# Where the load of w_out stands in GpSimd's queue of loads

## The chip, the cores and the metric

The kernel runs on one core of a Trainium2 chip. The metric is the time of one execution on the device, in microseconds (us). The median of three runs of the kernel before is 156.59 us, the lowest is 156.43 and the highest 156.64.

## The reference

An attention layer with a sliding window and four sink positions feeds a gated MLP block whose gate mixes along the sequence. There are 4 batches of 768 positions, 8 heads of 64 values, so 512 model columns, and twice 512 columns inside the MLP. Cut to what matters:

```python
scores = scale * (q @ k.T)                      # per batch and head, 768 x 768
keep = (pos_k < 4) | ((0 <= pos_q - pos_k) & (pos_q - pos_k < 128))
a = softmax(where(keep, scores, -1e9))
x = concat_heads(a @ v)                         # 768 x 512 per batch

h = gelu(x @ w_in)                              # 768 x 1024
u, v = h[:, :512], h[:, 512:]
v_n = (v - mean(v)) / sqrt(var(v) + 1e-6) * g_ln
v_s = w_sg @ v_n + b_sg[:, None]                # mixes the 768 positions
out = x + (u * v_s) @ w_out
```

## The kernel before

Everything is cut into 128 positions (a tile, six of them in a batch) and 128 columns. The four batches, numbered 0 to 3, go through the same steps, and the steps of neighbouring batches are interleaved by hand. The order is the string `STEPS`: the program walks through it, and each word calls the function of that name with the numbers behind the dots. The last letter, where there is one, is the engine: A for ScalarE (ACT), D for VectorE (DVE), P for GpSimd (POOL). A scheduler changes nothing of it. Each engine gets its own instructions in the order of the string, runs them strictly in that order, and waits on semaphores where an instruction needs something that another engine or a DMA has still to deliver.

These are the steps that the text speaks of. `b` is the batch, `p` a pair of heads (0 to 3).

- `LQ.b.t` and `LK.b.t` (issued in `load`, L223, for batches 1 and 2) load tile t of q or k of a batch, all heads: 1024 runs of 64 values, turned from float32 to bfloat16 on the way, 128 KB in SBUF. `LVH.b.i` (L269) loads v of four heads, 384 KB in SBUF. `LWO` (L283) loads all of w_out, 512 KB in SBUF, 512 runs of 512 values. All of these are issued by POOL and go through one software queue that the 16 DMA engines serve.
- `TQ.b.g` and `TK.b.g` (L377) turn two tiles of q or k on TensorE (PE); `EQ` and `EK` copy the result to SBUF. `TK.2.1` needs the key tiles `LK.2.2` and `LK.2.3`, `TQ.2.1` needs the query tiles `LQ.2.2` and `LQ.2.3`, `TK.2.2` needs `LK.2.4` and `LK.2.5`.
- `QK.b.p.g` (L478) makes scores on PE, `EX.b.p.g` (L483) takes their exponential on ACT, `MK.b.p.g` masks the result: one multiplication on DVE (L490), or two selections on POOL (L493 and L496).
- `AV.b.p.k` (L519, L523, L526) multiplies the masked weights by v for one half of the positions. For batch 1, `AV.1.p.1` covers tiles 3, 4 and 5 with five matmuls each; from tile 4 on it reads what `MK.1.p.2` has masked. `NR` (L535, L536) divides by the sums.
- `SP`, `GT` and `GM` (L622, L627, L632) make the gate; `GM.0.1.2.P` is one of its products on POOL.
- `OU.b.t` (L639) is the last matmul of a tile and the only reader of w_out. `OU.0.0` is the first of them. `RA` adds x to it on DVE, `ST` stores the sum.

The tile framework gives POOL's loads eight completion semaphores in turn, and a load waits at its issue until the load that used its semaphore before has landed. That is the eighth POOL load before it. As long as the loads before it land in time, nobody sees this wait.

In the part of the string around the change, each of the engines concerned has this order before the change:

- POOL: `LK.2.1 LVH.1.0 LVH.1.1 LQ.2.2 LWO LK.2.2 LK.2.3 LQ.2.3 LQ.2.4 LQ.2.5 GM.0.0.2 LK.2.4 LK.2.5 MK.1.1.2 MK.1.0.2 MK.1.2.2 MK.1.3.2 GM.0.1.2 LK.3.0 GM.0.1.3 GM.0.1.1 LVH.2.0 ...`
- PE, from its 52nd microsecond on: `... AV.1.2.0 AV.1.3.0 QK.2.0.0 QK.2.1.0 OU.0.0 TK.2.1 AV.1.0.1 AV.1.1.1 AV.1.2.1 AV.1.3.1 QK.2.2.0 QK.2.3.0 OU.0.1 OU.0.2 TK.2.2 TQ.2.1 TQ.2.2 MV.1.0 ...`

Of the kernel before, what the change touches and what calls it, by code (L numbers as in the profile page):

```python
# [30 lines left out]
WE.0.A WT.1 GV.0.2 LK.1.5 TK.1.1 MU.0.2 LB.P EK.1.1.A BN.0.2 Z.0.0.A LK.2.0 WT.2 GU.0.2 MU.0.0 WE.1.D RS.0.2 WE.2.D  # L31
Z.0.1.A LQ.2.0 NM.0.2 Z.0.2.A Z.0.3.D Z.0.4.D WT.3 LQ.2.1 WT.4 GU.0.0 WE.3.D WT.5 LQ.1.4 Z.0.5.D TQ.1.1 QK.1.0.0
EQ.1.1.D QK.1.1.0 LQ.1.5 SP.0.0.0 WE.4.D LK.2.1 EX.1.0.0 VSM.1 SP.0.0.1 WE.5.D EX.1.1.0 LVH.1.0 GT.0.0.0 TK.1.2 KS.1
GT.0.0.1 QK.1.2.0 QK.1.3.0 EX.1.2.0 SP.0.0.2 LVH.1.1 GM.0.0.0.D EX.1.3.0 MK.1.2.0.D TQ.2.0 EK.1.2.A LQ.2.2 QK.1.0.1
EQ.2.0.D QK.1.1.1 TQ.1.2 EX.1.0.1 GT.0.0.2 LWO SP.0.0.3 EQ.1.2.D EX.1.1.1 LK.2.2 MK.1.0.1.D TK.2.0 MK.1.0.0.D QK.1.2.1
LK.2.3 EK.2.0.A QK.1.3.1 MK.1.3.0.D SK.1.0 GM.0.0.1.D LQ.2.3 SP.0.1.0 EX.1.2.1 GT.0.0.3 MK.1.1.0.D LQ.2.4 EX.1.3.1
SP.0.1.1 MK.1.1.1.D LQ.2.5 MK.1.2.1.D SX.1.0 QK.1.0.2 QK.1.1.2 GT.0.1.0 EX.1.0.2 GM.0.0.2.P SP.0.1.2 GT.0.1.1 EX.1.1.2
LK.2.4 GM.0.1.0.D AV.1.0.0 MK.1.3.1.D AV.1.1.0 LK.2.5 GM.0.0.3.D QK.1.2.2 GT.0.1.2 QK.1.3.2 EX.1.2.2 SP.0.1.3 NR.1.0.0
MK.1.1.2.P EX.1.3.2 NR.1.1.0 AV.1.2.0 AV.1.3.0 MK.1.0.2.P GT.0.1.3 QK.2.0.0 QK.2.1.0 NR.1.2.0 EX.2.0.0 OU.0.0
MK.1.2.2.P NR.1.3.0 TK.2.1 RA.0.0 AV.1.0.1 XD.1.0 EK.2.1.A MK.1.3.2.P AV.1.1.1 NR.1.0.1 AV.1.2.1 EX.2.1.0 GM.0.1.2.P  # L40
NR.1.1.1 AV.1.3.1 NR.1.2.1 QK.2.2.0 LK.3.0 QK.2.3.0 EX.2.2.0 OU.0.1 NR.1.3.1 GM.0.1.3.P EX.2.3.0 OU.0.2 XD.1.1 RA.0.1
GM.0.1.1.P TK.2.2 MK.2.3.0.D TQ.2.1 LVH.2.0 TQ.2.2 EQ.2.1.D MV.1.0 EQ.2.2.D LQ.3.0 EK.2.2.D LQ.3.1 VSM.2 MU.1.0 GV.1.0
# [668 lines left out]
```

## Time and profile before

| | |
|---|---|
| median of 3 runs | 156.59 us |
| the profiled execution | 157.69 us |
| its span, first instruction to last | 156.0 us |
| PE busy | 146.7 us, 94% of the span |
| DVE, ACT, POOL busy | 123.4, 99.0, 99.3 us |
| granted TensorE clock | 9 tenths or more in each of 40 slices |
| software queue's share of 16 DMA engines | 94.9% |
| share of w_out's load in the chain that ended last | 7% |

The profile is of one execution. Times in it count from the start of its span, and 1.69 us of the execution lie outside that span. PE's busy time is modelled for the ends of its matmuls, so a PE that is busy is not a PE at its peak. The page lists, for groups of instructions, the idle time of the engine just before them and what ended it; the chain of waits goes back from the last instruction to whatever released each one.

### The profile page before, as it was taken

To read this page: it belongs to the slowest core of one execution; us is meant where nothing else is said; L and a number is where in the kernel's file an instruction comes from. 1 tells how busy PE (TensorE), PEld (TensorE's weight loads), DVE (VectorE), ACT (ScalarE), POOL (GpSimd) and SP (SyncE) were. 2 spreads that over 40 slices of the span, in tenths; PEclk is the share of its full clock that TensorE was granted. 3 is DMA by queue.
4 is the path that set the end of the run, shared out by engine and by line. 5 is a ranking of instruction groups with operands and counts; after the bars stand their busy time and mean duration, and the time that the engine had idled before them with its cause. 6 is when DMAs were issued, how large, how long until landed. Compare 5 with 4: busy or idle time off the path is not lost.

```text
span 156.0 us, 3856 instructions
## 1 busy us (share of the span) xinstructions
PE 146.7 (94%) x1549; PEld 94.2 (60%) x1549; DVE 123.4 (79%) x295; ACT 99.0 (64%) x110; POOL 99.3 (64%) x127
## 2 busy tenths in 40 slices
PE   6988989999999979989999999999999999999990
PEld 2445577779675756747566764486567644776530
DVE  4557789829989969969789887899789956867981
ACT  3699798799899846276897855269954025591000
POOL 4099779388999899997549869640798610300400
PEclk9999999999999999999999999999999999999999
DMA  4999999999999999999999199995710580510064
GB/s 156 282 365 151 153 197 189 166 192 193 146 143 142 193 152 139 167 156 156 168 230 246 22 285 174 178 197 60 236 71 3 102 235 0 202 63 11 0 227 179
DMA packets 86170, 24.67 MB, mean 158 GB/s; under 512 B 78660, under 2 KB 83016, under 8 KB 86152
## 3 DMA queue, kind: packets, MB, share of 16 engines
q0 software_dynamic: 64608, 11.01, 94.9%
q1 hardware_dynamic: 21544, 13.41, 33.1%
q8 instruction: 12, 0.20, 0.5%
q14 instruction: 6, 0.05, 0.1%
HBM read 24.81 MB, written 6.29 MB: 199 GB/s over the span
## 4 chain that ended last, share of the span: by engine, by line
PE 73%; DMA 17%; DVE 2%; POOL 2%; issue 1%; ACT 1%; SPq 1%; ACTq 0%
PE mm L622 17%; PE mm L639 14%; PE sc L561 13%; PE sc L602 12%; DMA w_out_sb<-in_moe_w_out_dram 7%; DMA v_sb<-in_v_dram 6%; PE sc L478 4%; DMA uT<-in_k_dram 4%; PE mm L519 3%; PE mm L377 3%; PE mm L523 2%; PE mm L526 2%; PE mm L614 1%; POOL v_sb L269 1%; PE mm L545 1%
## 5 line engine op out<-in xcount | busy, mean ns | idle before, releaser
L483 ACT ACTIVATE P<-sc 128x1024 bf16<-128x1024 f32 (+1 forms) x48 | 43.4, 953 | 10.3 <-PE sc L478 10.1
L622 PE MATMUL mm<-wsgT,z 128*128 128x384 bf16 x192 | 34.1, 327 | 0.0
L622 PEld LDWEIGHTS <-z 128*128 128x128 bf16 x192 | 17.7, 98 | 11.9 <-issue 0.7
L639 PE MATMUL mm<-w_out_sb,wsg_gated 128*128 128x512 bf16 x96 | 22.7, 379 | 1.1 <-DMA w_out_sb<-in_moe_w_out_dram 1.1
L561 PE MATMUL sc<-w_in_sb,xT 128*128 128x512 bf16 x96 | 22.2, 379 | 0.7 <-ACT vt L565 0.7
L627 DVE SCALAR_TENSOR_TENSOR gtmp<-mm,g_sb,b_bc 128x384 bf16<-128x384 f32 x32 | 19.1, 611 | 4.2 <-PE mm L622 3.6
L602 PE MATMUL sc<-xT,w_in_sb 128*128 128x256 bf16 x192 | 22.1, 273 | 0.0
L493 POOL TENSOR_SCALAR_AFFINE_SELECT P<-P 128x512 bf16<-128x512 bf16 x21 | 14.0, 667 | 12.3 <-ACT P L483 12.0
L632 POOL TENSOR_TENSOR wsg_gated<-gtmp,uT 128x384 bf16<-128x384 bf16 x15 | 14.5, 982 | 10.9 <-DVE gtmp L627 10.9
L574 DVE BATCH_NORM_STATS2 st<-vt 128x6 f32<-128x512 f32 x24 | 15.4, 685 | 7.5 <-ACT vt L565 7.4
L602 PEld LDWEIGHTS <-w_in_sb 128*128 128x128 bf16 x192 | 18.7, 98 | 3.0
L536 DVE TENSOR_TENSOR x_sb<-mm,rcp 128x384 bf16<-128x384 f32 (+1 forms) x36 | 18.5, 513 | 1.2
L643 DVE TENSOR_TENSOR ot<-mm,x_sb 128x512 f32<-128x512 f32 x24 | 16.1, 684 | 2.7 <-PE mm L639 2.5
L565 ACT ACTIVATE vt<-sc 128x1024 f32<-128x1024 f32 x12 | 12.3, 1027 | 9.0 <-PE sc L561 8.9
L583 POOL TENSOR_TENSOR rs<-rs,neg_half 128x4 f32<-128x4 f32 (+1 forms) x8 | 6.9, 867 | 17.4 <-DVE rs L578 16.0
L223 POOL DMA_DIRECT2D k<-in_k_dram x18 | 16.4, 928 | 0.7 <-DMA v_sb<-in_v_dram 0.7
L223 POOL DMA_DIRECT2D q<-in_q_dram x18 | 16.7, 952 | 0.0
L519 PE MATMUL mm<-v_sb,P 128*128 128x65 bf16 x192 | 15.9, 194 | 0.7 <-DMA v_sb<-in_v_dram 0.6
L519 PEld LDWEIGHTS <-P 128*128 128x128 bf16 x192 | 14.5, 98 | 2.8 <-issue 0.6
L639 PEld LDWEIGHTS <-wsg_gated 128*128 128x128 bf16 x96 | 9.2, 98 | 11.4 <-DMA w_out_sb<-in_moe_w_out_dram 1.4
L561 PEld LDWEIGHTS <-xT 128*128 128x128 bf16 x96 | 9.2, 98 | 10.9 <-issue 0.9
L478 PE MATMUL sc<-qT,kT 64*128 64x128 bf16 (+1 forms) x256 | 14.8, 238 | 0.6 <-DVE qT L198 0.3
(90 smaller groups left out, 244.4 us busy)
## 6 DMA issues: line engine op xcount, KB each, us to landing
out_dram<-ot SPq DMA_DIRECT2D x24, 256.0 KB, 2.3
v_sb<-in_v_dram POOLq DMA_DIRECT2D x8, 384.0 KB, 8.3
q<-in_q_dram POOLq DMA_DIRECT2D x18, 128.0 KB, 6.7
k<-in_k_dram POOLq DMA_DIRECT2D x18, 128.0 KB, 6.9
wsg_gated<-in_moe_w_sg_dram POOLq DMA_DIRECT2D x2, 576.0 KB, 8.3
w_in_sb<-in_moe_w_in_dram POOLq DMA_DIRECT2D x2, 512.0 KB, 10.2
uT<-in_q_dram SPq DMA_DIRECT2D x2, 384.0 KB, 3.2
uT<-in_k_dram SPq DMA_DIRECT2D x2, 384.0 KB
```

Source lines behind the costliest of these rows:

```text
L223: return nc.gpsimd.dma_start(out=dst.rearrange("p (h d) -> p h d", h=H), in_=heads(src, b, i))
L478: nc.tensor.matmul(sc[:, hl, c:c + 128 * ni], at(kT, b)[rows, j, p, :], at(qT, b)[rows, i:i + ni, p, :], start=not biased, stop=(not biase ...
L483: nc.scalar.activation(out=P.new((b, p, g))[:, :, 0:w], in_=sc_ring[b, p, g][:, :, 0:w], func=AF.Exp, scale=scale)
L519: nc.tensor.matmul(av[:, il, hl, :], pt[:, hl, c:c + 128], vb[:, h, i, :], start=first, stop=False)
L536: nc.vector.tensor_mul(x_sb.get(b)[:, i0:i0 + n, 128 * p:128 * (p + 1)].rearrange("p t (h d) -> p t h d", h=2), av[:, :, :, 0:Dh], rcp[:, ...
L561: nc.tensor.matmul(hp[:, jl, :], xT[b][:, 2 * g + jl, c, :], w_in_sb[:, c, d_half:2 * d_half], start=(c == 0), stop=(c == KD - 1))
L574: nc.vector.bn_stats(out=sts[jl], in_=vt[b, g][:, jl, :])
L602: nc.tensor.matmul(hp[:, dc // 2, 256 * (dc % 2):256 * (dc % 2 + 1)], w_in_sb[:, c, 128 * dc:128 * (dc + 1)], xT[b][:, 2 * g:2 * g + 2, c, :],
L622: nc.tensor.matmul(ps[:, 0:NH], z[b][:, si, 128 * dc:128 * (dc + 1)], wsgT[:, si, NH * hf:NH * (hf + 1)], start=(si == 0), stop=(si == NT ...
L627: nc.vector.scalar_tensor_tensor(out=gtmp.new((b, hf, dc)), in0=mm_ring["g", b, hf, dc][:, 0:NH], scalar=g_sb[:, dc:dc + 1], in1=b_bc[:, N ...
L639: nc.tensor.matmul(ps, gated(b, hf)[:, dc, 128 * tl:128 * (tl + 1)], w_out_sb[:, dc, :], start=(dc == 0), stop=(dc == KU - 1))
L643: nc.vector.tensor_add(ot.new((b, t)), mm_ring["o", b, t], x_sb[b][:, t, :])
```

## The change

`LWO` moves up one load in POOL's queue, into the place of `LQ.2.2`. `LQ.2.2` moves down behind `LK.2.2` and `LK.2.3`. So POOL issues `LVH.1.1 LWO LK.2.2 LK.2.3 LQ.2.2 LQ.2.3 ...` where it issued `LVH.1.1 LQ.2.2 LWO LK.2.2 LK.2.3 LQ.2.3 ...`. The number of instructions stays the same on every engine, and the order stays the same on every engine but POOL. The rest of the diff is the new breaking of the lines.

```diff
-GT.0.0.1 QK.1.2.0 QK.1.3.0 EX.1.2.0 SP.0.0.2 LVH.1.1 GM.0.0.0.D EX.1.3.0 MK.1.2.0.D TQ.2.0 EK.1.2.A LQ.2.2 QK.1.0.1
-EQ.2.0.D QK.1.1.1 TQ.1.2 EX.1.0.1 GT.0.0.2 LWO SP.0.0.3 EQ.1.2.D EX.1.1.1 LK.2.2 MK.1.0.1.D TK.2.0 MK.1.0.0.D QK.1.2.1
-LK.2.3 EK.2.0.A QK.1.3.1 MK.1.3.0.D SK.1.0 GM.0.0.1.D LQ.2.3 SP.0.1.0 EX.1.2.1 GT.0.0.3 MK.1.1.0.D LQ.2.4 EX.1.3.1
+GT.0.0.1 QK.1.2.0 QK.1.3.0 EX.1.2.0 SP.0.0.2 LVH.1.1 GM.0.0.0.D EX.1.3.0 MK.1.2.0.D TQ.2.0 EK.1.2.A LWO QK.1.0.1
+EQ.2.0.D QK.1.1.1 TQ.1.2 EX.1.0.1 GT.0.0.2 SP.0.0.3 EQ.1.2.D EX.1.1.1 LK.2.2 MK.1.0.1.D TK.2.0 MK.1.0.0.D QK.1.2.1
+LK.2.3 LQ.2.2 EK.2.0.A QK.1.3.1 MK.1.3.0.D SK.1.0 GM.0.0.1.D LQ.2.3 SP.0.1.0 EX.1.2.1 GT.0.0.3 MK.1.1.0.D LQ.2.4
```

More of the change, by code (lines that the diff above doesn't have):

```diff
@@ L33 @@
 EQ.1.1.D QK.1.1.0 LQ.1.5 SP.0.0.0 WE.4.D LK.2.1 EX.1.0.0 VSM.1 SP.0.0.1 WE.5.D EX.1.1.0 LVH.1.0 GT.0.0.0 TK.1.2 KS.1
-GT.0.0.1 QK.1.2.0 QK.1.3.0 EX.1.2.0 SP.0.0.2 LVH.1.1 GM.0.0.0.D EX.1.3.0 MK.1.2.0.D TQ.2.0 EK.1.2.A LQ.2.2 QK.1.0.1
-EQ.2.0.D QK.1.1.1 TQ.1.2 EX.1.0.1 GT.0.0.2 LWO SP.0.0.3 EQ.1.2.D EX.1.1.1 LK.2.2 MK.1.0.1.D TK.2.0 MK.1.0.0.D QK.1.2.1
-LK.2.3 EK.2.0.A QK.1.3.1 MK.1.3.0.D SK.1.0 GM.0.0.1.D LQ.2.3 SP.0.1.0 EX.1.2.1 GT.0.0.3 MK.1.1.0.D LQ.2.4 EX.1.3.1
-SP.0.1.1 MK.1.1.1.D LQ.2.5 MK.1.2.1.D SX.1.0 QK.1.0.2 QK.1.1.2 GT.0.1.0 EX.1.0.2 GM.0.0.2.P SP.0.1.2 GT.0.1.1 EX.1.1.2
-LK.2.4 GM.0.1.0.D AV.1.0.0 MK.1.3.1.D AV.1.1.0 LK.2.5 GM.0.0.3.D QK.1.2.2 GT.0.1.2 QK.1.3.2 EX.1.2.2 SP.0.1.3 NR.1.0.0
-MK.1.1.2.P EX.1.3.2 NR.1.1.0 AV.1.2.0 AV.1.3.0 MK.1.0.2.P GT.0.1.3 QK.2.0.0 QK.2.1.0 NR.1.2.0 EX.2.0.0 OU.0.0
+GT.0.0.1 QK.1.2.0 QK.1.3.0 EX.1.2.0 SP.0.0.2 LVH.1.1 GM.0.0.0.D EX.1.3.0 MK.1.2.0.D TQ.2.0 EK.1.2.A LWO QK.1.0.1
+EQ.2.0.D QK.1.1.1 TQ.1.2 EX.1.0.1 GT.0.0.2 SP.0.0.3 EQ.1.2.D EX.1.1.1 LK.2.2 MK.1.0.1.D TK.2.0 MK.1.0.0.D QK.1.2.1
+LK.2.3 LQ.2.2 EK.2.0.A QK.1.3.1 MK.1.3.0.D SK.1.0 GM.0.0.1.D LQ.2.3 SP.0.1.0 EX.1.2.1 GT.0.0.3 MK.1.1.0.D LQ.2.4
+EX.1.3.1 SP.0.1.1 MK.1.1.1.D LQ.2.5 MK.1.2.1.D SX.1.0 QK.1.0.2 QK.1.1.2 GT.0.1.0 EX.1.0.2 GM.0.0.2.P SP.0.1.2 GT.0.1.1
+EX.1.1.2 LK.2.4 GM.0.1.0.D AV.1.0.0 MK.1.3.1.D AV.1.1.0 LK.2.5 GM.0.0.3.D QK.1.2.2 GT.0.1.2 QK.1.3.2 EX.1.2.2 SP.0.1.3
+NR.1.0.0 MK.1.1.2.P EX.1.3.2 NR.1.1.0 AV.1.2.0 AV.1.3.0 MK.1.0.2.P GT.0.1.3 QK.2.0.0 QK.2.1.0 NR.1.2.0 EX.2.0.0 OU.0.0
 MK.1.2.2.P NR.1.3.0 TK.2.1 RA.0.0 AV.1.0.1 XD.1.0 EK.2.1.A MK.1.3.2.P AV.1.1.1 NR.1.0.1 AV.1.2.1 EX.2.1.0 GM.0.1.2.P
```

## The prediction, made before the result was known

> **What bounds the kernel now.** I read the chain of waits first, then what PE waited for, then the stretch around w_out on POOL and PE. The chain by engine and line, from the page:
>
> ```profile
> PE 73%; DMA 17%; DVE 2%; POOL 2%; issue 1%; ACT 1%; SPq 1%; ACTq 0%
> ```
>
> The chain in order of time, from 43 to 58 us (columns: start, length, what):
>
> ```profile
> 44.65 0.78 POOL q L223
> 45.43 0.09 issue
> 45.52 10.79 DMA w_out_sb<-in_moe_w_out_dram
> 56.31 0.05 issue
> 56.35 1.04 PE mm L639 x4
> ```
>
> The load of w_out is issued at 45.52, behind the issue of LQ.2.2, lands at 56.31, and OU.0.0 starts at once. What PE waited for from 56 us to the end:
>
> ```profile
> PE mm L639 <- DMA w_out_sb<-in_moe_w_out_dram: 1.1, 1, 1.1
> PE sc L561 <- ACT vt L565: 0.7, 1, 0.7
> ```
>
> PE stood still 1.15 us for w_out (55.20 to 56.35) and 0.70 us for a step that itself follows PE's own work; otherwise it is busy to the end. So a microsecond that PE loses or wins at 55 to 60 us should reach the end whole. What is late there besides w_out is seen on POOL (start, length, engine, line, operation, count, idle before and its releaser):
>
> ```profile
> 52.40 1.82 POOL L223 DMA_DIRECT2D k<-in_k_dram  x2 [0.72 <-DMA v_sb<-in_v_dram]
> 54.22 0.66 POOL L493 TENSOR_SCALAR_AFFINE_SELECT P<-P 128x512 bf16<-128x512 bf16 x1
> ...
> 58.35 0.63 POOL L496 TENSOR_SCALAR_AFFINE_SELECT P<-P 128x512 bf16<-128x512 bf16 x1
> 58.96 0.90 POOL L632 TENSOR_TENSOR wsg_gated<-gtmp,uT 128x384 bf16<-128x384 bf16 x1
> ```
>
> The first line is LK.2.4 (52.40) and LK.2.5 (53.34). LK.2.4 waited for v, LVH.1.1, which is the eighth load of POOL before it: this is the semaphore that it takes over. Behind LK.2.5 come eight selections, MK.1.1.2, MK.1.0.2, MK.1.2.2, MK.1.3.2, and the last ends at 58.98. PE's timeline shows who needs that:
>
> ```profile
> 59.29 0.19 PE L519 MATMUL mm<-v_sb,P 128*128 128x65 bf16 x1
> ...
> 59.46 0.19 PE L519 MATMUL mm<-v_sb,P 128*128 128x65 bf16 x1
> ```
>
> AV.1.3.1 begins at 59.29 with tile 3 and at 59.46 with tile 4, the first to read MK.1.3.2; its weights are loaded at 59.41. So MK.1.3.2 is only 0.40 us ahead of its reader, in a run in which PE had been held 1.15 us by w_out.
>
> **When w_out lands after the change.** The issue moves from 45.52 to 44.65. That alone is worth nothing: the queue is backed up, and loads land 7 to 10 us behind their issue. What counts is the work taken out from ahead of it. LQ.2.2 is one of six equal loads; those landing in a row behind w_out (LK.2.2 56.52, LK.2.3 57.34, then 58.18, 59.01, 59.90, 60.74) stand 0.84 us apart. LQ.2.2 itself landed only 0.26 us behind LVH.1.1 (52.12 and 51.86), the lower bound for what it takes. I use 0.84, because six landings agree on it, and because LVH.1.1's writes were slow at the end (mean 48 ns instead of 32) while the queue moved the same number of packets per microsecond.
>
> But w_out's landing is not one time. The trace holds the sixteen increments of its semaphore, one from each DMA engine: fourteen lie between 53.25 and 54.20, the fifteenth at 54.71, and the last, alone, at 56.31. Before that, at LQ.2.2, no DMA engine was that far behind (51.01 to 52.12, evenly spread). In between there is something else on the DMA engines, seen between 53.9 and 55.4 us:
>
> ```profile
> q8 instruction: 1, 0.02, 4.2%
> ```
>
> It is one 16 KB fetch of instructions at 54.28 that took 1.02 us. I read it so: it came between w_out's data and w_out's increment on one DMA engine, and from there on that engine stays 1.0 us behind the others through LK.2.4. The fetch follows the program's progress, which up to 55 us doesn't depend on w_out, so it stays at 54.28. With 0.84 us less ahead of w_out, that engine has passed on its increment before the fetch begins. I expect the landing at 54.71 - 0.84 = 53.87; bounds are 53.36 (54.20 - 0.84) and 55.47 (56.31 - 0.84, if the straggler comes along).
>
> On this the Trainium skill has two rules that pull apart. "DMA: Bandwidth & Descriptors", Queues, rings and completion order, says that the increment lands only after every earlier write of its DMA engine, across queues; that fits a fetch in between, and by it the sum is mine. The same page, Latency and other measured facts, says that two of the sixteen DMA engines are usually slower; by that the straggler belongs to the load and comes along, which is the second rival below. The even spread at 51 to 52 us speaks for the first.
>
> **What this removes on PE.** OU.0.0 no longer waits and starts at 55.20, 1.15 us earlier. TK.2.1 follows 0.88 us later (57.23 against 56.35), at 56.08, and needs LK.2.2 and LK.2.3: 57.34 - 0.84 = 56.50 for the latter, which holds TK.2.1's second half by about 0.2 us. AV.1.0.1 could start near 56.8 instead of 57.67, 0.9 us earlier. Then the masks set the pace: even with POOL as it was, AV.1.3.1 couldn't start tile 4 more than 0.40 us earlier. So the gain is capped at 0.40 us, not at 1.15.
>
> **What it adds on POOL.** The eighth load before LK.2.5 was LQ.2.2, landed at 52.12, and LK.2.5 followed LK.2.4 without a pause. After the change the eighth before is LWO. LK.2.5 can be issued only when w_out has landed, at 53.87 instead of being ready at 53.34. To this comes POOL's restart: LK.2.4 was released at 51.86 (its semaphore instruction ran at 51.88) and started at 52.40, 0.54 later, the one case here of a POOL load that really waited. The other bound is the start of POOL's cast at 7.93, 0.09 after the landing at 7.84. I take 0.52, since that is the same instruction behind the same wait. LK.2.5 then starts at 53.87 + 0.52 = 54.39, which is 1.05 us later than 53.34. With 0.09 it is 53.96, 0.62 later.
>
> Queued behind LK.2.5 are the eight selections (0.59 us from one to the next, nothing idle between them), so all four masks shift by 1.05: MK.1.0.2 ends near 57.6, MK.1.3.2 near 60.03. AV.1.0.1 waits for its mask around 57.6 (0.25 earlier than the 57.86 of before for that tile); AV.1.3.1 reaches its mask at 60.03 + 0.08 = 60.11 instead of 59.46. PE loses 1.05 - 0.40 = **0.65 us**, and the 1.15 us won at OU.0.0 is given back as a wait inside the AVs. With the short restart it is 0.62 - 0.40 = 0.22 us.
>
> **What costs nothing, and its cover.** The LQ.2.2 that lands later, near 57.3, is read by TQ.2.1 at 62.5: 5 us of cover. LK.2.5's landing at 61.76 is set by the backlog of the queue until 60.74 and not by its issue; TK.2.2 starts at 62.09, and its second half reads it at 62.3. POOL's later work slides by 1.05 us: GM.0.1.2 and its like are needed by OU.0.3 at 75 us, the loads of batch 3 and v of batch 2 land 5 us and more ahead of use, and at 71.5 to 72.6 POOL idles 1.09 us waiting for DVE, which takes up the shift. The new eighth loads of LWO, LK.2.2 and LK.2.3 had landed by 42.4 us, before any of them is issued; those of LK.3.0 and later land 2 us or more before. EK.2.1 comes earlier on ACT and the sum of OU.0.0 earlier on DVE, neither on the path. If the cover at TK.2.2 were gone it would cost what LK.2.5 is late, a few tenths.
>
> **Sum.** The profiled execution took 157.69 us, 156.0 of span and 1.69 around it, 1.10 above the median of 156.59. Its stage at 52 to 60 us shifts by +0.65, nothing later takes it back, so I expect 158.3 for a profiled execution and 156.59 + 0.65 = 157.24 for the median.
>
> **The rivals.**
> 1. *Faster: the masks stay in place.* If w_out lands early enough that LK.2.5 isn't held (52.8 with the long restart, 53.25 with the short one), PE wins the capped 0.40 us: 156.2. For it: fourteen of sixteen increments would lie between 52.4 and 53.36. Against it: the last one counts, and the fifteenth at 54.71 has no fetch of this size to blame. It decides at a landing below 53.3. 0.12.
> 2. *Much slower: the straggler comes along,* because that DMA engine is slow by itself, or the fetch moves. The landing is 55.47, LK.2.5 starts at 55.99, 2.65 late, and PE loses 2.25: 158.8. If only LQ.2.2's 0.26 us were saved, it would be 2.8 and 159.4. 0.10.
> 3. *A wash.* Between the two: the short restart (+0.22), or a landing at 53.36 with the long one (53.88, 0.54 late, +0.14). The stall moves from w_out to the masks, and the time stays: 156.8. 0.18.
>
> **How the numbers follow.** The forecast, a loss of 0.3 to 1.1 us, has the remaining 0.60. A measurement of this kernel can tell about 0.2% from no change, 0.31 us. Faster by more than that is rival 1, nearly whole: 0.11. Within it are the wash and the edges of its neighbours: 0.22. Slower: 0.67. The range runs from rival 1 to beyond the forecast's upper edge (a landing at 54.3 gives 1.1 us), and leaves out most of rival 2: 156.2 to 158.2. The likeliest case alone spans 156.9 to 157.7.
>
> **What would show it.** In the changed profile: w_out issued near 44.65 and landed near 53.9; no wait of PE for w_out; LK.2.5 with an idle time before it on POOL, released by w_out's load; the selections starting near 55.3 instead of 54.22; and a new wait of PE at L519 or L523 for POOL's masks, some 0.6 us in AV.1.0.1 and again at AV.1.3.1. I am wrong if LK.2.5 shows no idle time ahead of it, if w_out lands after 55, or if PE's shift at AV.1.3.1 is taken back before the end.

## The result: slower, by the wait that took the place of the one removed

The changed kernel takes 158.16 us in the median (157.39 to 160.22, 16 runs), the kernel before in the same series 156.62 (156.06 to 157.52, 16 runs). The ratio is 1.0084 with a 95% interval of 1.0065 to 1.0104, which is 1.0 to 1.6 us. A second series gave 1.0049 (1.0017 to 1.0081), 0.3 to 1.3 us. The ratios leave out executions that were slower at a lower granted clock: one of the changed kernel's 16, and four of the six of the last variant below, which took 161 to 163 us at 0.979 to 0.989.

What is new in the chain that ended last is POOL (chain by engine, from the page of the changed kernel):

```profile
PE 63%; DMA 16%; POOL 9%; DVE 3%; issue 3%; ACT 2%; SPq 1%; ACTq 0%
```

POOL had 2% of it before, PE 73%. In order of time the chain shows where it goes now (start, length, what):

```profile
43.65 9.41 DMA w_out_sb<-in_moe_w_out_dram
53.06 0.29 issue
53.35 0.87 POOL k L223
54.22 0.01 issue
54.23 0.66 POOL P L493
...
58.40 0.60 POOL P L496
59.00 0.05 issue
59.05 0.20 PE mm L523
```

w_out lands, and the next link isn't OU.0.0 but POOL's LK.2.5, then all eight selections, then AV.1.3.1. On POOL itself (start, length, engine, line, operation, idle before and its releaser):

```profile
51.72 0.94 POOL L223 DMA_DIRECT2D k<-in_k_dram  x1 [1.05 <-DMA v_sb<-in_v_dram]
53.35 0.87 POOL L223 DMA_DIRECT2D k<-in_k_dram  x1 [0.69 <-DMA w_out_sb<-in_moe_w_out_dram]
54.23 0.66 POOL L493 TENSOR_SCALAR_AFFINE_SELECT P<-P 128x512 bf16<-128x512 bf16 x1
```

LK.2.4 and LK.2.5 were one unbroken row before; now POOL stands idle for 0.69 us ahead of LK.2.5, until w_out has landed. This idle time is called the hold in what follows. What PE waited for between 50 and 70 us (total, times, longest):

```profile
PE mm L523 <- POOL P L496: 0.8, 2, 0.4
PE sc L561 <- ACT vt L565: 0.7, 1, 0.7
PE mm L377 <- DMA k<-in_k_dram: 0.2, 1, 0.2
```

The 1.1 us for w_out is gone. In its place are two waits for masks, in AV.1.0.1 and in AV.1.3.1, and a short one of TK.2.1 for LK.2.3. PE's timeline has the two:

```profile
56.70 0.20 PE L523 MATMUL mm<-v_sb,P 128*128 128x65 bf16 x1 [0.38 <-POOL P L496]
...
59.05 0.20 PE L523 MATMUL mm<-v_sb,P 128*128 128x65 bf16 x1 [0.39 <-POOL P L496]
```

The profiled execution of the changed kernel took 157.39 us with a span of 155.7, less than the 156.0 of before, and this needs care. Instruction by instruction, PE is 1.00 us earlier than before from 21 to 55 us, because the first loads came earlier in that execution (both loads of v for batch 0 landed 1.00 us earlier), and 0.43 us earlier from 60 us to the end, without change. So what happens at 55 to 60 us costs 0.57 us, and the rest is how the execution began. For that reason all profiles below are read from the start of EX.2.0.0 on ACT, the last exponential before OU.0.0, and "stage" is the time from there to the start of the last matmul with w_out. All figures but the stage are relative to that start, in us. "First mask" is the start of MK.1.1.2 on POOL.

| kernel | LVH.1.1 lands | LK.2.5 issued | w_out lands | first mask | EX.2.2.0 | stage |
|---|---|---|---|---|---|---|
| before | -3.22 | -1.75 | +1.22 | -0.87 | 5.21 | 96.38 |
| before, again | -2.78 | -1.31 | -0.12 | -0.43 | 5.21 | 96.38 |
| changed | -2.90 | -0.73 | -1.02 | +0.15 | 5.78 | 96.96 |
| changed, again | -3.15 | -0.07 | -0.36 | +0.81 | 6.46 | 97.64 |
| w_out ahead of LQ.2.2 only | -3.31 | -1.11 | -1.40 | -0.23 | 5.42 | 96.60 |
| LK.2.2 in the place of LQ.2.2 | -2.63 | -1.16 | +0.05 | -0.28 | 5.37 | 96.55 |
| changed, LK.2.5 behind two masks | -3.33 | +0.53 | -1.40 | -1.84 | 4.71 | 95.89 |
| the same, again | -3.10 | +0.75 | +0.41 | -1.62 | 4.92 | 96.27 |
| before, LK.2.5 behind two masks | -3.26 | +0.59 | -0.51 | -1.77 | 4.76 | 95.94 |
| as "behind two masks", MK.1.3.2 on DVE | -3.26 | +0.58 | -1.36 | -1.78 | 4.62 | 95.86 |

EX.2.2.0 is the first exponential behind the AVs and marks when PE has come through them. In five of the first six rows it follows the first mask by 5.63 to 5.65 us: the masks set the pace. The one exception is the first profile of before, 6.08, in which w_out did.

The table also separates the hold from another wait. In all ten profiles LK.2.4 is held by the same rule for LVH.1.1, so the masks also move with the landing of v. From that landing to the first mask it takes 2.35 us in each of the three rows where LK.2.5 stands ahead of the masks and isn't held (both of before, and LK.2.2 in the place of LQ.2.2). It takes 3.05, 3.96 and 3.08 us in the three rows with a hold, and the difference is the hold: 0.7, 1.6 and 0.7 us.

### The profile page after: what moved, and what is told of

It reads as the page before. It is cut to its first block, busy times and chain, and to the rows that moved or that the text cites. A ratio compares the mean times of both kernels' runs of the same rounds, so it can differ in the third digit from the quotient of the medians.

```text
span 155.7 us, 3855 instructions
## 1 busy us (share of the span) xinstructions
PE 147.1 (94%) x1549; PEld 94.2 (61%) x1549; DVE 122.8 (79%) x295; ACT 98.9 (64%) x110; POOL 99.7 (64%) x127
## 4 chain that ended last, share of the span: by engine, by line
PE 63%; DMA 16%; POOL 9%; DVE 3%; issue 3%; ACT 2%; SPq 1%; ACTq 0%
PE mm L622 15%; PE mm L639 13%; PE sc L561 12%; PE sc L602 10%; DMA v_sb<-in_v_dram 6%; DMA w_out_sb<-in_moe_w_out_dram 6%; PE sc L478 4%; DMA uT<-in_k_dram 4%; PE mm L519 3%; POOL q L223 2%; POOL v_sb L269 2%; PE mm L523 2%; POOL P L493 2%; POOL P L496 2%; PE mm L526 1%
## 5 line engine op out<-in xcount | busy, mean ns | idle before, releaser
L519 PE MATMUL mm<-v_sb,P 128*128 128x65 bf16 x192 | 16.4, 194 | 0.3 <-DMA v_sb<-in_v_dram 0.2
L523 PE MATMUL mm<-v_sb,P 128*128 128x65 bf16 x160 | 15.6, 194 | 0.8 <-POOL P L496 0.8
```

What stands on the lines that cost most here:

```text
L519: nc.tensor.matmul(av[:, il, hl, :], pt[:, hl, c:c + 128], vb[:, h, i, :], start=first, stop=False)
L523: nc.tensor.matmul(av[:, il, hl, :], pt[:, hl, c:c + 128], vb[:, h, i - 1, :], start=False, stop=(i < 2 and il == n - 1 and hl == 1))
```

## The experiments

**The changed kernel again.** No edit.

> The changed kernel a second time, for a second profile. Its profiled execution showed a stage loss of 0.57 us (every PE instruction from 60 us to the end is 0.43 us early against before, where up to 55 us they are 1.00 us early), while the medians are 1.5 us apart. Theory (hold only): the stage loss is 0.5 to 0.7 us in every execution, and the rest is a difference in the first 20 us or outside the span. Rival (straggler in some executions): the second profile, if its time is near the median of 158.2, shows w_out's last increment behind the 16 KB fetch, LK.2.5 started 2 us or more later than with the first, and a stage loss of 1.3 us or more.

The second execution took 158.63 us, and its stage 97.64, 1.26 more than before. POOL and PE in it:

```profile
52.09 0.94 POOL L223 DMA_DIRECT2D k<-in_k_dram  x1 [0.78 <-DMA v_sb<-in_v_dram]
54.63 0.88 POOL L223 DMA_DIRECT2D k<-in_k_dram  x1 [1.60 <-DMA w_out_sb<-in_moe_w_out_dram]
```

```profile
PE mm L519 <- POOL P L493: 0.8, 1, 0.8
PE mm L523 <- POOL P L496: 0.8, 2, 0.4
```

The hold is 1.60 us here instead of 0.69, since w_out landed 0.66 us later against the rest and LK.2.4 was issued 0.25 us earlier. So the loss isn't one number: it follows w_out's landing from one execution to the next. The theory that the loss is 0.5 to 0.7 in each falls. The rival is right on that, but not on the cause it named: the last two increments came at 53.94 and 54.34, before the 16 KB fetch began at 54.38. Its numbers are missed too, the loss of 1.3 us narrowly, and the 2 us for LK.2.5 clearly (0.66 later against the rest). The mean of the two stage losses, 0.58 and 1.26, is 0.92 us. That lies inside the interval of the second series (0.3 to 1.3 us) and just below that of the first (1.0 to 1.6). As far as two profiles can tell, the stage accounts for most of the loss; whether for all of it isn't shown.

**LK.2.5 behind two masks.** w_out is still the eighth load before LK.2.5, but the first two masks no longer stand behind it.

```diff
-AV.1.1.0 LK.2.5 GM.0.0.3.D ... MK.1.0.2.P GT.0.1.3
+AV.1.1.0 GM.0.0.3.D ... MK.1.0.2.P LK.2.5 GT.0.1.3
```

> The changed kernel, with LK.2.5 moved on POOL from ahead of the masks to behind MK.1.1.2 and MK.1.0.2. Theory (the wait of LK.2.5 for w_out holds the masks): the first two masks start when LK.2.4 is issued, LK.2.5 finds w_out landed and doesn't wait, MK.1.3.2 ends where it ended before, and PE wins the capped 0.40 us: 0.3 to 0.4 us faster than before, some 1.0 us faster in the stage than the changed kernel. Rival (the moved query load or w_out's place costs by contention, not by the hold): it stays as slow as the changed kernel, 1 us or more slower than before.

```profile
51.66 0.94 POOL L223 DMA_DIRECT2D k<-in_k_dram  x1 [0.59 <-DMA v_sb<-in_v_dram]
52.61 0.66 POOL L493 TENSOR_SCALAR_AFFINE_SELECT P<-P 128x512 bf16<-128x512 bf16 x1
...
54.98 0.89 POOL L223 DMA_DIRECT2D k<-in_k_dram  x1
```

The masks follow LK.2.4 at once, and LK.2.5 comes at 54.98 without idle time, w_out having landed at 53.05. The stage is 95.89, 1.07 and 1.75 us below the two of the changed kernel. The timings agree in direction: 0.9999 of before (0.9976 to 1.0022), where the changed kernel in the same series is at 1.0049. The loss goes when the masks no longer stand behind LK.2.5. This run alone doesn't say how much of that is the hold, because the move also takes LK.2.5's own 0.9 us out from ahead of the masks; the same move on the kernel before, further down, wins nothing in the timings. The gain of 0.49 in the stage over before doesn't show in the timings either, though their interval reaches down to a gain of 0.4 us.

**w_out ahead of LQ.2.2 only.**

```diff
-LWO QK.1.0.1 ... LK.2.3 LQ.2.2 EK.2.0.A
+LWO LQ.2.2 QK.1.0.1 ... LK.2.3 EK.2.0.A
```

> Half of the change: w_out ahead of LQ.2.2, but LQ.2.2 directly behind it and ahead of the two key tiles, as before. Theory: w_out is still the eighth load before LK.2.5, so the hold and the loss at the masks are those of the changed kernel (0.5 to 0.7 us in the stage); LK.2.3 lands 0.84 us later than in the changed kernel, near its landing of before, so TK.2.1 waits about 1 us for it, which the wait for the masks covers. Time as the changed kernel, within 0.3 us. Rival (the query's place behind the keys is what costs): time as before.

```profile
50.83 0.94 POOL L223 DMA_DIRECT2D k<-in_k_dram  x1 [0.61 <-DMA v_sb<-in_v_dram]
52.51 0.88 POOL L223 DMA_DIRECT2D k<-in_k_dram  x1 [0.73 <-DMA w_out_sb<-in_moe_w_out_dram]
```

```profile
PE mm L377 <- DMA k<-in_k_dram: 0.4, 1, 0.4
```

The hold is there, 0.73 us, with the query in its old place against the keys. The stage is 96.60, only 0.22 above before, less than the 0.5 expected, because v and w_out landed 0.4 us earlier in this execution than in the changed kernel's first; the timings give 1.0031 (1.0003 to 1.0059), which overlaps the changed kernel's interval in the same series (1.0017 to 1.0081). TK.2.1 waited 0.4 us for its key, not the 1 us expected.

**LK.2.2 in the place of LQ.2.2.** The other half: w_out stays second behind LVH.1.1, the query goes behind the keys, and the eighth load before LK.2.5 is a small one.

```diff
-EK.1.2.A LWO QK.1.0.1 ... EX.1.1.1 LK.2.2 MK.1.0.1.D
+EK.1.2.A LK.2.2 QK.1.0.1 ... EX.1.1.1 LWO MK.1.0.1.D
```

> w_out stays one load behind LVH.1.1, but the load ahead of it is now LK.2.2, and LQ.2.2 goes behind LK.2.3 as in the change. LK.2.5's eighth load is then LK.2.2, which lands near 52 us in the frame of before. Theory: no hold, w_out as late as before, PE waits for it as before; the moved query costs nothing, so the stage takes what it takes before (within 0.2 us) and the time is that of before. Rival (the query behind the keys costs by itself): slower than before by 0.5 us or more.

```profile
52.60 1.82 POOL L223 DMA_DIRECT2D k<-in_k_dram  x2 [1.11 <-DMA v_sb<-in_v_dram]
54.42 0.67 POOL L493 TENSOR_SCALAR_AFFINE_SELECT P<-P 128x512 bf16<-128x512 bf16 x1
```

```profile
PE mm L523 <- POOL P L496: 0.8, 2, 0.4
```

Both keys are again one unbroken row: LK.2.5 was issued at 53.53 while w_out was still on its way (landed 54.74). So it isn't the depth of the queue or w_out's size that holds LK.2.5, it is which load is the eighth before it. The time is that of before, 0.9993 (0.9965 to 1.0022), and the stage 96.55, within the 0.2 us expected: moving the query costs nothing that can be told. The wait forecast for PE was missed. It didn't wait for w_out, which landed 1.17 us earlier against the rest than in the first profile of before. It waited twice for masks, because LVH.1.1 landed 0.59 us later than there, and the masks came with it. That is also why this stage is hardly shorter than the 96.60 of the run with a hold: the hold shows in the time from v's landing to the first mask (2.35 against 3.08 us), and not in these two stages.

**The kernel before, with LK.2.5 behind two masks.** The same edit as in the second experiment, on the kernel before.

> The kernel before, with LK.2.5 behind MK.1.1.2 and MK.1.0.2, as in the second experiment. Theory: the masks weren't late in the kernel before, w_out was; so nothing is won, 0 to 0.1 us. With the changed order the same move won 1.0 us or more in the stage, so the two together say that the hold and nothing else was lifted there. Rival (moving the key is a gain by itself): 0.4 us faster than before.

The timings show nothing won, 1.0002 (0.9972 to 1.0032), but this interval reaches down to a gain of 0.4 us. The profile says 0.44 us in the stage (95.94), as the rival had it: w_out landed at -0.51, ahead of OU.0.0, and PE waited neither for it nor for a mask. So in this execution the rival is right; how often w_out lands that early isn't shown.

**LK.2.5 behind two masks, again.**

> The second experiment again, for a second profile and more timings. Its first profile showed the stage from EX.2.0.0 to the last OU at 95.89 us, 0.49 less than before (96.38), while the timings said no difference. Theory: the stage takes 95.8 to 96.0 us again, since w_out's landing is no longer awaited by anybody, and the timings differ from before by where w_out lands in the executions of before. Rival: the stage varies in this kernel too, by 0.3 us or more.

```profile
PE mm L639 <- DMA w_out_sb<-in_moe_w_out_dram: 0.3, 1, 0.3
PE mm L523 <- POOL P L496: 0.3, 1, 0.3
```

Here w_out's last increment came alone, 1.80 us behind the fifteenth, and even from its earlier place w_out was late for PE. The stage is 96.27, so the theory's 95.8 to 96.0 is missed and the rival is right: it varies by 0.38 in this kernel. The timings are 0.9989 (0.9963 to 1.0014).

**The kernel before again.** No edit; in the timings it is compared with itself.

> The kernel before again, for a second profile. Theory: how late w_out is differs between executions. The first profile had one increment alone at 56.31, 1.60 behind the fifteenth, and PE waited 1.15 us for it. If the 16 KB fetch caused that, an execution in which it falls elsewhere shows w_out landed about 1.6 us earlier, a wait of PE of 0 to 0.3 us, and a stage 0.4 us shorter (95.9 to 96.1 us instead of 96.38, since the masks then set the pace). Rival: the straggler is there again, and the stage takes 96.3 to 96.5 us.

```profile
PE mm L523 <- POOL P L496: 0.4, 1, 0.4
PE mm L377 <- DMA k<-in_k_dram: 0.3, 1, 0.3
```

No wait for w_out at all, and a wait for the masks instead. Its stage is 96.38 to the hundredth: w_out's landing was 1.34 us earlier against the rest, but LVH.1.1 landed 0.44 later, LK.2.4 was held by that, and the masks came 0.44 later. The theory had the wait for w_out right and the stage wrong; the rival's stage came without its straggler, w_out's last increment being 0.08 us behind the fifteenth. The ratio of the kernel to itself is 1.0022 (0.9996 to 1.0048), which is how far timings of one series can be off.

**MK.1.3.2 on DVE as well.** The second experiment with `MK.1.3.2.P` made `MK.1.3.2.D`.

> As the run with the key tile behind two masks, and MK.1.3.2 done by DVE (0.68 us there) instead of POOL, to lift the cap. Theory: with MK.1.2.2 ended near 57.8 and MK.1.3.2 done on DVE right behind the sum of OU.0.0, PE goes through the AVs without a wait; what is late next is LK.2.3 for TK.2.1 (0.2 us) and LK.2.5's landing for TK.2.2. 0.6 to 0.9 us faster than before. Rival: DVE, busy over nine tenths of 53 to 57 us, delays NR and OU, and the gain stays at 0.4 us or less.

The stage is 95.86, 0.03 below the second experiment and 0.52 below before: PE's wait for masks falls from 0.4 to 0.2 us. The 0.6 to 0.9 expected isn't there in the stage, and neither is the rival's 0.4 or less. Only two executions can be compared with before, too few for a ratio. They took 155.95 and 156.08 us, both below the lowest of the 26 of before in that series (156.26), so whether this variant is faster stays open. None of the others is faster than before by more than its interval.

## Why the prediction was right, and which of its terms were off

- **The mechanism** is as forecast and now shown: w_out becomes the eighth load before LK.2.5, the masks behind it move, and the wait for w_out comes back in the AVs. With a small load in the eighth place there is no hold and no loss in the timings; with w_out in that place the hold is there even if the query stays ahead of the keys; and moving LK.2.5 behind two masks takes the loss away.
- **"A microsecond that PE loses at 55 to 60 us should reach the end whole"** held: PE's instructions are 0.57 us later against the start of the stage at 60 us, and still 0.57 at the end.
- **The place on PE** held: OU.0.0 without a wait, TK.2.1 held 0.2 us by LK.2.3 (measured 0.18), waits at tile 4 of AV.1.0.1 and of AV.1.3.1. The two waits are 0.38 and 0.39 us, where some 0.6 each was forecast.
- **The sum** gave 0.65 us. The profiles give 0.58 and 1.26 by stage, the timings 1.3 and 0.8. In the first profile the first mask is 1.02 us later than before, against 1.05 forecast, and the slack taken off is 0.44, against 0.40. But not all of it is the change's: 0.69 is the hold, and 0.33 would have come without it, because LK.2.4 waited that much longer for v in that execution. That the shift came out within 0.03 us is luck: in the frame of before LK.2.5 starts at 54.36 against 54.39 forecast, because a landing forecast 0.20 us too early and a restart 0.23 us too long cancel. In the second profile the shift of the first mask is 1.68 us.
- **The restart, 0.52 us, was mis-sized.** It is 0.29 in all three profiles with a hold (53.35 behind 53.06, 54.63 behind 54.34, 52.51 behind 52.22). The 0.54 of LK.2.4 is there again (51.72 behind 51.18), and in its case a separate semaphore instruction stands ahead of the load; LK.2.5 carries its wait itself. So LK.2.4 wasn't "the same instruction behind the same wait". Whether the semaphore instruction makes the difference wasn't tried.
- **The landing, 53.87, was too early for both profiles of the changed kernel, and taken as one number.** In the frame of before (55.09 added to the table's figures) these two have it at 54.07 and 54.73, and the four variants with w_out ahead of the query at 53.69, 53.69, 55.50 and 53.73. The 0.84 us for the query is about right for the bulk: the median increment comes 2.0 to 2.1 us before EX.2.0.0 in the two profiles of the changed kernel and 1.3 to 1.4 before it in both of the kernel before, so 0.7 us. It is the last increment that scatters, 0.06 to 1.80 us behind the fifteenth in ten profiles.
- **The fetch as the cause of the straggler isn't borne out.** In one profile two stragglers come before it begins (54.38), in two others it begins before the last increment and there is none (0.08 and 0.09 us behind the fifteenth). In two more there is one behind the fetch's start, 0.73 and 1.80 us behind the fifteenth, but it landed before the fetch had ended (54.74 against 54.83, 54.94 against 55.06); only in the first profile of before did it land after that. What makes the last increment late stays open. So the second rival was right that the straggler may come along. Its landing of 55.47 was met once (55.50), but in a variant where the first two masks don't stand behind LK.2.5, so its price of 2.25 us wasn't measured; the changed kernel's worse profile lost 1.26.
- **The premise was weaker than it looked.** That PE waits 1.15 us for w_out is true of one execution of before; in another it didn't wait at all, and the masks set the pace. The page of one execution named a bound that the next one didn't have. The size was forecast too small: 0.65 us, where the two series give 1.3 and 0.8. By the medians the loss is 1.54 us, above the 0.3 to 1.1 us that were forecast, and 158.16 lies only 0.04 us inside the range. That the range holds is in part luck. One reason can be seen, landings later than 53.87; whether the slack of one execution of before also misled the sum isn't shown.

## What to carry to other kernels

When a load is moved in a queue, ask not only when it lands but who takes over its completion semaphore: a load some places further down may be held by it, with everything that stands behind it on the issuing engine. A large load belongs where the load that follows it by that distance has nothing urgent behind it; here, moving that load behind the urgent work costs one word. And before a wait is priced from one profile, a second profile of the same kernel shows whether it is there at all.

## What the runs showed of the hardware that was not expected

- POOL started LK.2.5, which carries its wait itself, 0.29 us after the landing that it waited for (three profiles), and LK.2.4, which has a semaphore instruction ahead of it, 0.53 to 0.54 us after (ten profiles). Neither figure varied by more than 0.01 us.
- A load's sixteen increments can differ by far more than its size explains: w_out's last one lay 0.06 to 1.80 us behind the fifteenth, without a pattern by kernel.
- Two executions of one kernel can have the same stage to 0.01 us with different bounds (w_out in one, v by way of LK.2.4 and the masks in the other).
